# A retention layer and a gated FFN on one core: heads of odd pairs change places, and the products of the carried state go in two parts

## The chip, the cores and the metric

The kernel runs on one core of a Trainium2 chip. The metric is the device time of one launch in microseconds, as the median of several runs. The core has a matrix engine (TensorE, PE in the profile, with PEld for its weight loads), VectorE (DVE), ScalarE (ACT), GpSimd (POOL) and the sync engine (SP), which issues all transfers of this kernel on one queue that 16 DMA engines serve.

## The reference

Four sequences of 768 tokens, eight heads of 64 values. Each head carries a 64x64 state that decays by a fixed factor per token; the output of all heads, side by side, is the input x of a multiplicative FFN.

```python
q, k, v: (4, 8, 768, 64)          # batch, heads, tokens, head size
gamma = 1.0 - 2.0 ** (-5.0 - np.arange(H))
for t in range(S):
    state = gamma * state + outer(k[:, :, t], v[:, :, t])
    y[:, :, t] = scale * (q[:, :, t] @ state)
x = y.transpose(0, 2, 1, 3).reshape(B * S, H * D)      # 3072 x 512
a = x @ w1;  b = x @ w2                                # 512 x 1024 each
out = ((a * b) @ w3) @ w_out                           # 1024 x 1024, 1024 x 512
```

## The kernel before, in words

The tokens are cut into 12 stages of 256 (`n`), three to a sequence. W3 and w_out don't depend on the tokens, so the kernel first multiplies them into one 1024x512 matrix (`W3O`, functions `turn_w3`, `w3_mm`, `w3_out`). Everything is computed in float16 with float32 sums in PSUM.

A stage does this, and each step is a function. `load` brings Q, K and V of a stage into one of 15 staging buffers; `cast` and `cast_v` turn them into float16 (ScalarE the queries, GpSimd or VectorE the rest) and put a decay factor into V. Keys and queries are turned by TensorE in stages 0 to 2 and by a DMA transpose later (`dma_turn`, from stage 5 on `turn_pair` with both in one). `scores` are keys times queries inside chunks (two of 128 tokens in stages 0 and 1, four of 64 after), and `mask` cuts them to the causal part on VectorE. `kv` are keys times values, from which `state` makes the carried state at the start of each chunk, `TS[n, c]`. `inter` multiplies the carried state by the queries, and `av` adds scores times values to the same PSUM banks `X[n, 0]` and `X[n, 1]`. `x_out` takes them out with a decay factor into `XT[n]`, x transposed: row block `a` of 128 rows holds the pair of heads 2a and 2a+1. The FFN then computes `two_blocks` with W1 (`a_evac`, ScalarE) and W2 (`b_evac`, VectorE, which multiplies the two into `HT`), and `o_unit` multiplies `HT` by `W3O`; `o_copy` and `o_store` bring the result out. In stages 0 and 1 `rows` does the same as `two_blocks` in the order in which the blocks of W1 and W2 arrive.

All small products of a stage are 64x64: a product that reads its operands from partitions 0 to 63 or 64 to 127 uses the upper or lower half of TensorE's rows, and one that writes PSUM partitions 0 to 63 or 64 to 127 uses the left or right half of its columns. So there are four quarters. In `scores`, `kv` and `av` four products in a row lie on four quarters (`QUARTERS`). In `inter` before, the head r = 0 or 1 of a pair gives both halves (`X[n, g][half(r), ...]` from `TS[n, c][half(r), ...]`), so that two of the four quarters are in use. [...] In `inter` both row halves write both banks; in `av` row half g writes bank g. Between them stands `fence`: ScalarE reads a few elements of each bank, and `av` waits for it. From stage 4 on, the scores and keys-values of the next stage lie between `inter` and `av` of this one and cover that time.

The order on each engine is the order in which the program names the operations. It is written out by hand up to stage 3 (lines 588 to 853), with a loop after it (lines 902 to 942). A transfer whose staging buffer is in use, or whose semaphore still counts the transfer eight issues earlier, waits at the head of SP's queue, with all behind it.

Of the kernel before, what the change touches and what calls it, by code (L numbers as in the profile page):

```python
# [20 lines left out]
def kernel(  # L21
# [18 lines left out]
    PAIR = 3 + 2  # L40
# [15 lines left out]


# [62 lines left out]
    fetch(  # L120
        "r4 wo0 r1 r2 wo1 r5 wo2 r3 r6 k0 r7 wo3 q0 v0 r0 q1 k1 v1 w11 w13 w10 w12 w22 w23 w21 w20 "
        "v2 v3 k2 q2 k3 v4 q4"
    )
# [15 lines left out]
    def numbers():  # L139
# [6 lines left out]
        for h in range(H):  # L146
            r = (h % 2) * 64
            nc.gpsimd.memset(LGH[:, h : h + 1], -math.log(gam[h]))
            nc.gpsimd.memset(LGP[r : r + 64, h // 2 : h // 2 + 1], math.log(gam[h]))
# [73 lines left out]
    w3h, w3p, w3t, acc = {}, {}, {}, {}  # L223
# [23 lines left out]
    def w3_mm(f, i, tag=None, first=False, last=False):  # L247
        if first:
            acc[f] = bank(tag, [128, DM])
        for r in range(2):  # L250
# [6 lines left out]
    def w3_out(f, eng):  # L257
        copy(eng, W3O[f][:, :], acc.pop(f)[:, :])
# [116 lines left out]
    def kv(n, tags):  # L375
        last = n % PER == PER - 1
        if n < EO:
# [3 lines left out]
        for a in range(NP):  # L381
# [19 lines left out]

    def state(n, i, eng="g"):
        cs = chunks(n)
        if i == len(cs) and n % PER == PER - 1:
            return
# [22 lines left out]
    def inter(n, tags):  # L428
        begun = set()
        for g in range(2):  # L430
            X[n, g] = bank(tags[g], [128, NP, 128])
        cs = chunks(n)
        for a in range(NP):
            for c in cs:
                if (n, c) not in TS:
                    continue
                for r in range(2):
                    if n < EO:
                        g, o, rhs = c, X[n, c][half(r), a, :], qT[n][half(r), :, a, half(c)]
                    else:  # L440
                        s, g = c
                        o, rhs = X[n, g][half(r), a, s * 64 : (s + 1) * 64], qchunk(n, r, a, s, g)
                    nc.tensor.matmul(  # L443
                        o, lhsT=TS[n, c][half(r), a, :], rhs=rhs, start=((g, r) not in begun), stop=False,
                        skip_group_check=True,
                    )
                    begun.add((g, r))
        X[n] = begun

    def fence(n):  # L450

        for g in range(2):
            if (g, 0) in X[n]:
                s0 = 0 if n < EO or (n, (0, g)) in TS else 1
                t = att.tile([128, NP, 2 - s0], FP, tag=f"fence{g}", name="fence")
                nc.scalar.copy(t[:, :, :], X[n, g][:, :, :].rearrange("p a (s i) -> p a s i", s=2)[:, :, s0:, 0])  # L456

    def av(n):
        begun = X.pop(n)
        for a in range(NP):  # L460
            for t in range(2):
                for g, r in QUARTERS:
                    h = 2 * a + r
                    if n < EO:
                        o, rhs = X[n, g][half(r), a, :], am[n, a // 2, r][half(g), a % 2, t, :]
                    else:
                        o, rhs = X[n, g][half(r), a, t * 64 : (t + 1) * 64], am[n, None, r][half(g), a, t, :]
                    nc.tensor.matmul(  # L468
                        o, lhsT=v16[n][half(g), t, h * D : (h + 1) * D], rhs=rhs,
                        start=((g, r) not in begun), stop=(n >= EO or t == 1), skip_group_check=True,  # L470
                    )
                    begun.add((g, r))

    def x_out(n, g):
        if n not in XT:
# [19 lines left out]
    HT, pa = {}, {}  # L495

    def two_blocks(W, n, u, tag):
        ps = bank(tag, [128, 2, T])
# [13 lines left out]
    def b_evac(n, u, ps):  # L512
        if n not in HT:
            HT[n] = fsb.tile([128, 8, T], HP, tag="ht", name="ht", bufs=2)
        tt("v", HT[n][:, 2 * u : 2 * u + 2, :], pa.pop((n, u))[:, :, :], ps[:, :, :], MULT)
# [7 lines left out]
    rows_ps = {}  # L523

    def rows(W, n, uh, d, tags=None, first=False, last=False):

        w = "a" if W is W1 else "b"
        if first:
            rows_ps[w, n, uh] = [bank(t, [128, 2, T]) for t in tags]
        for j in range(4):  # L530
# [6 lines left out]
    def rows_out(w, n, uh, u, eng="s"):  # L537
        ps = rows_ps[w, n, uh][u]
# [7 lines left out]
    def o_unit(n, tb, tags, cuts=((0, 512),)):  # L546
        for (c0, c1), tag in zip(cuts, tags):
# [8 lines left out]
    o_sb = {}  # L556

    def o_copy(n, tb, c0=0, c1=512):
        if n not in o_sb:
            o_sb[n] = fsb.tile([128, 2, DM], FP, tag="osb", name="osb", bufs=3)  # L560
        nc.scalar.activation(o_sb[n][:, tb, c0:c1], o_ps.pop((n, tb, c0, c1))[:, :], AF.Copy, scale=final_scale)  # L561

    def o_store(n, tb, c0=0, c1=512):
        r0 = n * T + tb * 128
        nc.sync.dma_start(out[r0 : r0 + 128, c0:c1], o_sb[n][:, tb, c0:c1])  # L565

    def o_store_all(n):
        nc.sync.dma_start(
# [18 lines left out]
    ab = {}  # L587
    warm(8)
# [84 lines left out]
    w3_out(7, "s")  # L673
    turn("q", 1, "S1")
    mask(0, 1, 0)
    w3_out(6, "s")
    inter(0, ("S0", "X1"))
    cast("k", 1, "g")
    state(0, 2)
    fence(0)  # L680
    turned_w3(0, "v")
    av(0)
# [26 lines left out]
    inter(1, ("S1", "X0"))  # L709
    state(1, 2)  # L710
    rows(W1, 0, 1, 3)
    fence(1)
    state(1, 3)
    cast_w(W1, "w1", 2, "s")
    av(1)
    rows(W1, 0, 0, 0)
# [65 lines left out]
    inter(2, ("S1", "X0"))  # L782
    o_copy(0, 1)
    dma_turn("k", 3)
    fetch("q3 k4")
# [4 lines left out]
    fence(2)  # L790
    mask(2, 1)
    av(2)
# [10 lines left out]
    ab["a", 2, 0] = two_blocks(W1, 2, 0, "S1")  # L803
    o_copy(1, 1)
    state(3, 3)
    ab["a", 2, 1] = two_blocks(W1, 2, 1, "X0")
    state(3, 4)
    a_evac(2, 0, ab["a", 2, 0])
    cast("q", 3, "g")
    ab["a", 2, 2] = two_blocks(W1, 2, 2, "S0")  # L810
    a_evac(2, 1, ab["a", 2, 1])
# [4 lines left out]
    ab["a", 2, 3] = two_blocks(W1, 2, 3, "S1")  # L816
    a_evac(2, 2, ab["a", 2, 2])
    ab["b", 2, 0] = two_blocks(W2, 2, 0, "S0")
    cast("k", 4, "v")
    a_evac(2, 3, ab["a", 2, 3])  # L820
    ab["b", 2, 3] = two_blocks(W2, 2, 3, "S1")
    dma_turn("k", 4)
    fetch("q5 k5 v5")
    b_evac(2, 0, ab["b", 2, 0])
    ab["b", 2, 2] = two_blocks(W2, 2, 2, "X0")
    b_evac(2, 3, ab["b", 2, 3])
    ab["b", 2, 1] = two_blocks(W2, 2, 1, "S0")
    b_evac(2, 2, ab["b", 2, 2])
    inter(3, ("S1", "X1"))
    b_evac(2, 1, ab["b", 2, 1])  # L830
    scores(3, ("X0", "K"))
    fence(3)
# [5 lines left out]
    state(4, 2)  # L838
    av(3)
# [14 lines left out]

    LAST = 3

    def casts(n):
        if n < NS:  # L860
            cast("k", n, "g")
            cast_v(n, "g")

    def cast_queries(n):
        if n < NS:
            cast("q", n, "s")

    def turns(n):
        if n < NS:
            turn_pair(n)  # L870

    def loads(n):
        if n < NS:
            load("k", n)
            load("q", n, nc.sync)
            load("v", n, nc.sync)

    def catch_up(u):
        if u == 0:
            load("k", LAST + 3)  # L880
            turns(LAST + 2)
            o_store(2, 1)
            o_store(1, 1)
            o_store(2, 0)
            load("q", LAST + 3)
            load("v", LAST + 3)
        elif u == 1:
            load("k", LAST + 4)
        elif u == 3:
            casts(LAST + 3)  # L890

    def ahead(n):
        scores(n, ("S0", "S1"))
        kv(n, ("K", "F1"))

    def ahead_out(n):
        states(n)
        mask(n, 0)
        mask(n, 1)

    LATE = ()
    for n in range(LAST, NS):
        nxt = n + 1 < NS and n > LAST
        late = nxt and n in LATE
        if n > LAST:
            inter(n, ("X0", "X1"))
            fence(n)
            if nxt and not late:
                ahead(n + 1)
            av(n)  # L910
            x_out(n, 0)
            x_out(n, 1)
            if nxt and not late:
                ahead_out(n + 1)
            cast_queries(n + 2)
            turns(n + 2)
            if n == LAST + 1:
                load("q", n + 3)
                load("v", n + 3)
            loads(n + 4)  # L920
            casts(n + 3)
            o_unit(n - 1, 0, ("F2",))
            o_copy(n - 1, 0)
            o_unit(n - 1, 1, ("F0",))
            o_copy(n - 1, 1)
            o_store_all(n - 1)
        tags = ("F2", "F0", "X1" if late else "F1")
        for u in range(4):
            if late and u == 2:
                ahead(n + 1)  # L930
                for i in range(1, 4):
                    state(n + 1, i)
# [45 lines left out]
```

## Time and profile before

| | |
|---|---|
| median of 3 runs | 192.08 us (191.68 to 193.73) |
| span of the profiled execution | 190.6 us |
| PE busy | 174.9 us, 92% |
| PEld busy | 125.2 us, 66% |
| DVE busy | 100.6 us, 53% |
| ACT busy | 71.1 us, 37% |
| POOL busy | 50.5 us, 26% |
| moved by DMA | 40.75 MB, 214 GB/s in the mean |

The profile is one execution. The time of a run is longer than its span by launch and completion. Engine lines give a start and a length in microseconds, the engine, the line of the kernel, the operation with what it writes and reads, and how often it stands in a row; in brackets follows how long the engine stood idle before it and what ended that. In the chain, "DMA x" is a transfer from its issue to its landing. A busy PE is not a PE at its peak, since products overlap; so rates are read from the distance between starts.

### The profile page before, as it was taken

The page shows a single profiled execution, that of the slowest core. Times are in us where ns is not written, and L with a number is a line of the kernel's source. Part 1 is how long each engine was busy: PE and PEld are TensorE (multiplying, and loading weights), DVE is VectorE, ACT ScalarE, POOL GpSimd, SP SyncE. Part 2 cuts the span into 40 slices and gives each one's busy share as a digit, 9 for nine tenths or more (in the row PEclk, how much of TensorE's full clock was granted, in tenths as well). Part 3 has the DMA queues.
Part 4 walks back from the last instruction along what each step waited for, and adds up shares of the span by engine and source line. Part 5 has one row for each costly group of instructions (what it writes and reads, how often), then busy time and mean ns, then how long its engine had stood idle before and what let it go on. Part 6 is the DMA issues. An engine that isn't in the chain of part 4 may idle for free.

```text
span 190.6 us, 5952 instructions
## 1 busy us (share of the span) xinstructions
PE 174.9 (92%) x2592; PEld 125.2 (66%) x2592; DVE 100.6 (53%) x171; ACT 71.1 (37%) x131; POOL 50.5 (26%) x79
## 2 busy tenths in 40 slices
PE   7499998999999884899899969999999999999993
PEld 2254554788757652686785846868868688585872
DVE  2435788526866285538248427474384653744130
ACT  5634434462255202231534333343432432322322
POOL 7852237633230301020505233323033010000000
PEclk9979999999999999699999999999999999999999
DMA  5999999989998998999999999999998270030303
GB/s 218 399 407 357 321 290 381 413 210 235 234 212 185 206 246 179 223 252 241 203 219 193 291 198 243 237 246 229 216 292 215 39 185 3 0 115 0 108 6 110
DMA packets 83402, 40.75 MB, mean 214 GB/s; under 512 B 61232, under 2 KB 77872, under 8 KB 83376
## 3 DMA queue, kind: packets, MB, share of 16 engines
q1 hardware_dynamic: 83376, 40.38, 85.6%
q8 instruction: 20, 0.33, 0.8%
q14 instruction: 6, 0.05, 0.1%
HBM read 29.36 MB, written 6.29 MB: 187 GB/s over the span
## 4 chain that ended last, share of the span: by engine, by line
PE 57%; DMA 22%; SPq 6%; POOL 6%; issue 3%; DVE 2%; ACT 2%; POOLq 0%; DVEq 0%
PE psF L502 29%; PE psF L550 15%; DMA st<-in_k_dram 6%; DMA st<-in_v_dram 5%; DMA st<-in_moe_w_dram 4%; DMA st<-in_q_dram 4%; SPq L87 4%; DMA kqT<-kq 3%; PE psX L443 2%; PE psX L252 2%; PE psS L252 2%; SPq L565 1%; PE psX L468 1%; PE psS L353 1%; POOL v L62 1%
## 5 line engine op out<-in xcount | busy, mean ns | idle before, releaser
L502 PEld LDWEIGHTS <-w 128*128 128x128 f16 x640 | 63.3, 99 | 15.7 <-issue 5.8
L502 PE MATMUL psF<-xt,w 128*128 128x256 f16 x576 | 65.9, 276 | 4.0 <-ACT osb L561 4.0
L62 DVE TENSOR_TENSOR ht<-pa,psF 128x512 f16<-128x512 f32 x39 | 26.8, 687 | 42.3 <-PE psF L502 42.3
L550 PE MATMUL psF<-w3o,ht 128*128 128x512 f16 (+2 forms) x176 | 38.3, 370 | 0.0
L59 ACT COPY pa<-psF 128x512 f32<-128x512 f32 x39 | 22.7, 585 | 41.3 <-PE psF L502 36.6
L550 PEld LDWEIGHTS <-ht 128*128 128x128 f16 x200 | 18.4, 98 | 19.3
L62 POOL TENSOR_TENSOR v<-st,VN 128x1024 f16<-128x1024 f32 x8 | 15.2, 1902 | 33.3 <-DMA st<-in_v_dram 23.6
L561 ACT ACTIVATE osb<-psF 128x512 f32<-128x512 f32 (+2 forms) x22 | 12.6, 576 | 24.3 <-PE psF L550 24.3
L485 DVE TENSOR_TENSOR xt<-psX,YN 128x512 f16<-128x512 f32 x18 | 12.2, 725 | 8.8 <-PE psX L468 8.8
L532 PEld LDWEIGHTS <-w 128*128 128x128 f16 x128 | 12.1, 98 | 2.9 <-ACT w L59 1.3
L62 POOL TENSOR_TENSOR t<-s,GS 128x256 f16<-128x256 f32 x8 | 5.8, 726 | 30.5 <-DVE s L62 30.5
L252 PEld LDWEIGHTS <-w3t 128*128 128x128 f16 x64 | 5.8, 101 | 7.3 <-ACT w3t L59 1.6
L370 DVE TENSOR_TENSOR am<-psS,keep 128x512 f16<-128x512 f32 x15 | 9.6, 681 | 1.2 <-PE psX L353 1.2
L59 ACT CAST kq<-st 128x1024 f16<-128x1024 f32 x7 | 7.3, 1046 | 6.7 <-DMA st<-in_q_dram 6.7
L532 PE MATMUL psF<-xt,w 128*128 128x256 f16 x56 | 9.7, 273 | 0.0
L59 POOL CAST kq<-st 128x1024 f16<-128x1024 f32 x6 | 6.2, 1036 | 12.2 <-DMA st<-in_k_dram 12.2
L443 PEld LDWEIGHTS <-t 64*64 64x64 f16 x320 | 6.2, 109 | 3.1 <-issue 3.0
L240 PEld LDWEIGHTS <-w3h 128*128 128x128 f16 x64 | 4.4, 110 | 4.5 <-DVE w3h L59 3.5
L532 PE MATMUL psX<-xt,w 128*128 128x256 f16 x32 | 6.1, 273 | 0.8 <-ACT w L59 0.8
L502 PE MATMUL psS<-xt,w 128*128 128x256 f16 x48 | 5.7, 272 | 1.0 <-DVE ht L62 1.0
L468 PE MATMUL psX<-am,v 64*64 64x64 f16 (+1 forms) x320 | 6.0, 197 | 0.5 <-ACT fence L456 0.5
L468 PEld LDWEIGHTS <-v 64*64 64x64 f16 x384 | 5.0, 106 | 1.8 <-issue 0.9
(137 smaller groups left out, 201.3 us busy)
## 6 DMA issues: line engine op xcount, KB each, us to landing
st<-in_moe_w_dram SPq DMA_DIRECT2D x16, 512.0 KB, 8.9
st<-in_q_dram SPq DMA_DIRECT2D x12, 512.0 KB, 6.6
st<-in_v_dram SPq DMA_DIRECT2D x20, 256.0 KB, 5.9
st<-in_k_dram SPq DMA_DIRECT2D x20, 256.0 KB, 5.4
out_dram<-osb SPq DMA_DIRECT2D x8, 512.0 KB, 5.0
st<-in_moe_w_out_dram SPq DMA_DIRECT2D x4, 512.0 KB, 7.3
out_dram<-osb SPq DMA_DIRECT2D x7, 256.0 KB, 3.8
st<-in_k_dram SPq DMA_DIRECT2D x2, 512.0 KB, 10.1
```

The lines of the kernel that those rows point to most:

```text
L59: {"v": nc.vector.tensor_copy, "g": nc.gpsimd.tensor_copy, "s": nc.scalar.copy}[eng](dst, src)
L62: (nc.vector if eng == "v" else nc.gpsimd).tensor_tensor(dst, a, b, op)
L87: via.dma_start(t[:, s * 512 : (s + 1) * 512].rearrange("p (h d) -> p h d", d=D), src[:, s * 128 : (s + 1) * 128, :].rearrange("h i d -> i ...
L252: nc.tensor.matmul(acc[f][:, :], lhsT=w3t[f][:, g * 128 : (g + 1) * 128], rhs=WO[i][:, r, :], start=(first and r == 0), stop=(last and r = ...
L370: nc.vector.tensor_tensor(t[:, :, :, :].rearrange("p a s i -> p (a s) i"), ps[:, :, :, :].rearrange("p a s i -> p (a s) i"), keep64[:, :]. ...
L443: nc.tensor.matmul(o, lhsT=TS[n, c][half(r), a, :], rhs=rhs, start=((g, r) not in begun), stop=False, skip_group_check=True,)
L468: nc.tensor.matmul(o, lhsT=v16[n][half(g), t, h * D : (h + 1) * D], rhs=rhs, start=((g, r) not in begun), stop=(n >= EO or t == 1), skip_g ...
L485: nc.vector.tensor_tensor(XT[n][:, :, :].rearrange("p a (s x) -> p (a s) x", s=2)[:, :, g * 64 : (g + 1) * 64].rearrange("p k (i t) -> p k ...
L502: nc.tensor.matmul(ps[:, i, :], lhsT=W[d][:, f * 128 : (f + 1) * 128], rhs=XT[n][:, d, :], start=(i == 0 and d == 0), stop=(i == 1 and d = ...
L532: nc.tensor.matmul(rows_ps[w, n, uh][j // 2][:, j % 2, :], lhsT=W[d][:, f * 128 : (f + 1) * 128], rhs=XT[n][:, d, :], start=(first and j % ...
L550: nc.tensor.matmul(ps[:, :], lhsT=HT[n][:, f, tb * 128 : (tb + 1) * 128], rhs=W3O[f][:, c0:c1], start=(f == 0), stop=(f == 7),)
L561: nc.scalar.activation(o_sb[n][:, tb, c0:c1], o_ps.pop((n, tb, c0, c1))[:, :], AF.Copy, scale=final_scale)
```

## The change

Heads of odd pairs change places in the output. `place(a, r)` gives the half in which head r of pair a lies: its own for even a, the other for odd a. `inter` and `av` write there, `numbers` fills the decay table of x accordingly, and rows of W1 and W2 have to follow: blocks 1 and 3 (which multiply row blocks 1 and 3 of x) are loaded with their two halves exchanged, as two transfers of 64 rows.

`inter` is split into parts 0 and 1. In part 0 bank g takes its products from row half 1-g, in part 1 from row half g, as in `av`. So the fence moves between the two parts. It reads one element of one half of each bank. Within a part, the even and the odd pair together touch all four quarters. From stage 4 on the order is part 0, fence, half of the next stage's `kv`, its `scores`, the other half of `kv`, part 1, `av`. In stages 0 and 1 other products lie between the parts (in stage 0 the transposes of the queries of stage 1, in stage 1 two groups of `rows`), in stage 2 the scores and one output product, in stage 3 the scores, the keys-values of stage 4 and an output product. In the last stage the first output product of stage 10, now in two cuts of 320 and 192 columns, lies between them.

The output tiles of stages 0 and 1 are put into the buffers of the float16 w_out, and the loop is written out line by line. Apart from the lines shown, the order of the operations is kept.

```diff
+    def place(a, r):
+        return r ^ (a % 2)
...
+    def load_heads(src, i):
+        if i % 2 == 0:
+            return load_rows(src, i)
+        t = new_stage()
+        for r in range(2):
+            r0 = i * 128 + (1 - r) * 64
+            nc.sync.dma_start(t[r * 64 : (r + 1) * 64, :], src[r0 : r0 + 64, :])
+        return t
...
-                w_st[kind, i] = load_rows({"w1": moe_w1, "w2": moe_w2}[kind], i)
+                w_st[kind, i] = load_heads({"w1": moe_w1, "w2": moe_w2}[kind], i)
...
-    def kv(n, tags):
+    def kv(n, tags, parts=(0, 1)):
...
-        for a in range(NP):
+        for a in range(2 * parts[0], 2 * parts[-1] + 2):
...
+    def inter(n, part, tags=None):
...
+        for i in range(NP // 2):
+            for s in range(1 if n < EO else 2):
+                for a in (2 * i, 2 * i + 1):
+                    for g in range(2):
+                        c = g if n < EO else (s, g)
+                        if (n, c) not in TS:
+                            continue
+                        r = g ^ 1 ^ part
+                        o = place(a, r)
+                        if n < EO:
+                            dst, rhs = X[n, g][half(o), a, :], qT[n][half(r), :, a, half(c)]
+                        else:
+                            dst, rhs = X[n, g][half(o), a, s * 64 : (s + 1) * 64], qchunk(n, r, a, s, g)
+                        nc.tensor.matmul(
+                            dst, lhsT=TS[n, c][half(r), a, :], rhs=rhs, start=((g, o) not in begun), stop=False,
+                            skip_group_check=True,
+                        )
+                        begun.add((g, o))
...
     def fence(n):
-
         for g in range(2):
-            if (g, 0) in X[n]:
-                s0 = 0 if n < EO or (n, (0, g)) in TS else 1
-                t = att.tile([128, NP, 2 - s0], FP, tag=f"fence{g}", name="fence")
-                nc.scalar.copy(t[:, :, :], X[n, g][:, :, :].rearrange("p a (s i) -> p a s i", s=2)[:, :, s0:, 0])
+            if (g, g) in X[n]:
+                t = att.tile([128, 1], FP, tag=f"fence{g}", name="fence")
+                nc.scalar.copy(t[half(g), :], X[n, g][half(g), NP - 1, 64:65])
...
+    inter(4, 0, ("X0", "X1"))
+    fence(4)
+    kv(5, ("K", "F1"), (0,))
+    scores(5, ("S0", "S1"))
+    kv(5, ("K", "F1"), (1,))
+    inter(4, 1)
+    av(4)
...
+    inter(11, 0, ("X0", "X1"))
+    fence(11)
+    o_unit(10, 0, ("F2",), ((0, 320),))
+    o_copy(10, 0, 0, 320)
+    o_unit(10, 0, ("F1",), ((320, 512),))
+    inter(11, 1)
+    av(11)
+    o_copy(10, 0, 320, 512)
+    x_out(11, 0)
+    x_out(11, 1)
+    o_unit(10, 1, ("F0",))
```

More of the change, by code (lines that the diff above doesn't have):

```diff
@@ L426, in states @@
             state(n, i, eng)
-    def inter(n, tags):
-        begun = set()
-        for g in range(2):
[L431 to L448, printed above, removed]
@@ L673 @@
     w3_out(7, "s")
+    inter(0, 0, ("S0", "X1"))
+    fence(0)
     turn("q", 1, "S1")
@@ L892, in ahead @@
[L892 to L932, printed above, removed]
-                mask(n + 1, 0)
-            a_unit(n, u, tags[2 * u % 3])
-            b_unit(n, u, tags[(2 * u + 1) % 3])
-            if late and u == 2:
-                mask(n + 1, 1)
-            if late and u == 2 + 1:
-                state(n + 1, 4)
-                state(n + 1, 5)
-            if n == LAST:
-                catch_up(u)
@@ new lines @@
+    evac("a", 3, 2)
+    blk("b", 3, 2, "F1")
+    evac("b", 3, 2)
+    blk("a", 3, 3, "F2")
+    evac("a", 3, 3)
+    blk("b", 3, 3, "F0")
+    evac("b", 3, 3)
+    cast("k", 6, "g")
+    cast_v(6, "g")
+    inter(4, 0, ("X0", "X1"))
[5 more added lines that the diff above has]
+    av(4)
+    x_out(4, 0)
+    x_out(4, 1)
+    state(5, 1)
+    state(5, 2)
+    state(5, 3)
+    state(5, 4)
+    state(5, 5)
+    mask(5, 0)
@@ new lines @@
+    evac("a", 4, 2)
+    blk("b", 4, 2, "F1")
+    evac("b", 4, 2)
+    blk("a", 4, 3, "F2")
+    evac("a", 4, 3)
+    blk("b", 4, 3, "F0")
+    evac("b", 4, 3)
+    inter(5, 0, ("X0", "X1"))
+    fence(5)
+    kv(6, ("K", "F1"), (0,))
+    scores(6, ("S0", "S1"))
+    kv(6, ("K", "F1"), (1,))
+    inter(5, 1)
+    av(5)
+    x_out(5, 0)
+    x_out(5, 1)
+    state(6, 1)
+    state(6, 2)
+    state(6, 3)
+    state(6, 4)
+    state(6, 5)
+    mask(6, 0)
+    mask(6, 1)
+    cast("q", 7, "s")
+    turn_pair(7)
@@ new lines @@
+    evac("a", 5, 3)
+    blk("b", 5, 3, "F0")
+    evac("b", 5, 3)
+    inter(6, 0, ("X0", "X1"))
+    fence(6)
+    kv(7, ("K", "F1"), (0,))
+    scores(7, ("S0", "S1"))
+    kv(7, ("K", "F1"), (1,))
+    inter(6, 1)
+    av(6)
+    x_out(6, 0)
+    x_out(6, 1)
+    state(7, 1)
+    state(7, 2)
+    state(7, 3)
+    state(7, 4)
+    state(7, 5)
+    mask(7, 0)
+    mask(7, 1)
+    cast("q", 8, "s")
+    turn_pair(8)
+    load("k", 10)
+    load("q", 10)
+    load("v", 10)
+    cast("k", 9, "g")
@@ new lines @@
+    inter(7, 0, ("X0", "X1"))
+    fence(7)
+    kv(8, ("K", "F1"), (0,))
+    scores(8, ("S0", "S1"))
+    kv(8, ("K", "F1"), (1,))
+    inter(7, 1)
+    av(7)
+    x_out(7, 0)
+    x_out(7, 1)
+    state(8, 1)
+    state(8, 2)
+    state(8, 3)
+    state(8, 4)
+    state(8, 5)
+    mask(8, 0)
+    mask(8, 1)
+    cast("q", 9, "s")
+    turn_pair(9)
+    load("k", 11)
+    load("q", 11)
+    load("v", 11)
+    cast("k", 10, "g")
+    cast_v(10, "g")
+    o_unit(6, 0, ("F2",))
+    o_copy(6, 0)
@@ new lines @@
+    o_unit(6, 1, ("F0",))
+    o_copy(6, 1)
+    o_store_all(6)
+    blk("a", 7, 0, "F2")
+    evac("a", 7, 0)
+    blk("b", 7, 0, "F0")
+    evac("b", 7, 0)
+    blk("a", 7, 1, "F1")
+    evac("a", 7, 1)
+    blk("b", 7, 1, "F2")
+    evac("b", 7, 1)
+    blk("a", 7, 2, "F0")
+    evac("a", 7, 2)
+    blk("b", 7, 2, "F1")
+    evac("b", 7, 2)
+    blk("a", 7, 3, "F2")
+    evac("a", 7, 3)
+    blk("b", 7, 3, "F0")
+    evac("b", 7, 3)
+    inter(8, 0, ("X0", "X1"))
+    fence(8)
+    kv(9, ("K", "F1"), (0,))
@@ new lines @@
+    scores(9, ("S0", "S1"))
+    kv(9, ("K", "F1"), (1,))
+    inter(8, 1)
+    av(8)
+    x_out(8, 0)
+    x_out(8, 1)
+    state(9, 1)
+    state(9, 2)
+    state(9, 3)
+    state(9, 4)
+    state(9, 5)
+    mask(9, 0)
+    mask(9, 1)
+    cast("q", 10, "s")
+    turn_pair(10)
+    cast("k", 11, "g")
+    cast_v(11, "g")
+    o_unit(7, 0, ("F2",))
+    o_copy(7, 0)
+    o_unit(7, 1, ("F0",))
+    o_copy(7, 1)
+    o_store_all(7)
+    blk("a", 8, 0, "F2")
+    evac("a", 8, 0)
+    blk("b", 8, 0, "F0")
@@ new lines @@
+    evac("b", 8, 0)
+    blk("a", 8, 1, "F1")
+    evac("a", 8, 1)
+    blk("b", 8, 1, "F2")
+    evac("b", 8, 1)
+    blk("a", 8, 2, "F0")
+    evac("a", 8, 2)
+    blk("b", 8, 2, "F1")
+    evac("b", 8, 2)
+    blk("a", 8, 3, "F2")
+    evac("a", 8, 3)
+    blk("b", 8, 3, "F0")
+    evac("b", 8, 3)
+    inter(9, 0, ("X0", "X1"))
+    fence(9)
+    kv(10, ("K", "F1"), (0,))
+    scores(10, ("S0", "S1"))
+    kv(10, ("K", "F1"), (1,))
+    inter(9, 1)
+    av(9)
+    x_out(9, 0)
+    x_out(9, 1)
@@ new lines @@
+    state(10, 1)
+    state(10, 2)
+    state(10, 3)
+    state(10, 4)
+    state(10, 5)
+    mask(10, 0)
+    mask(10, 1)
+    cast("q", 11, "s")
+    turn_pair(11)
+    o_unit(8, 0, ("F2",))
+    o_copy(8, 0)
+    o_unit(8, 1, ("F0",))
+    o_copy(8, 1)
+    o_store_all(8)
+    blk("a", 9, 0, "F2")
+    evac("a", 9, 0)
+    blk("b", 9, 0, "F0")
+    evac("b", 9, 0)
+    blk("a", 9, 1, "F1")
+    evac("a", 9, 1)
+    blk("b", 9, 1, "F2")
+    evac("b", 9, 1)
+    blk("a", 9, 2, "F0")
+    evac("a", 9, 2)
@@ new lines @@
+    blk("b", 9, 2, "F1")
+    evac("b", 9, 2)
+    blk("a", 9, 3, "F2")
+    evac("a", 9, 3)
+    blk("b", 9, 3, "F0")
+    evac("b", 9, 3)
+    inter(10, 0, ("X0", "X1"))
+    fence(10)
+    kv(11, ("K", "F1"), (0,))
+    scores(11, ("S0", "S1"))
+    kv(11, ("K", "F1"), (1,))
+    inter(10, 1)
+    av(10)
+    x_out(10, 0)
+    x_out(10, 1)
+    state(11, 1)
+    state(11, 2)
+    state(11, 3)
+    state(11, 4)
+    state(11, 5)
+    mask(11, 0)
+    mask(11, 1)
+    o_unit(9, 0, ("F2",))
+    o_copy(9, 0)
```

350 lines of the change are left out of this document (267 added, 83 removed).

## The prediction

> **What bounds the kernel now.** I read the chain of work that ended last first, then the 40 slices, then the timelines of TensorE and of the DMA queue. The chain (start, us, what):
>
> ```profile
> 25.05 7.52 DMA st<-in_moe_w_dram
> 32.59 1.05 ACT w L59
> 33.69 0.39 PE psX L532 x2
> ...
> 43.46 5.80 DMA st<-in_k_dram
> ...
> 68.37 7.07 DMA st<-in_q_dram
> ...
> 90.87 0.60 ACT osb L561
> 91.51 7.15 PE psF L502 x64
> ...
> 106.55 6.21 DMA kqT<-kq
> 112.81 0.45 PE psS L353 x32
> 113.52 0.27 PE psX L468 x32
> 113.79 3.56 PE psF L550 x16
> 117.34 6.99 PE psF L502 x64
> 124.33 0.56 PE psX L443 x28
> ```
>
> Until 112.81 us the chain returns to a transfer again and again: a block of W1, K, Q, and last the transposed keys and queries of stage 7, for which TensorE stands 1.67 us. From there to 187 us it runs on TensorE alone, in a period of 12 us: the products of the carried state (L443), scores (L353), keys-values (L392), `av` (L468), the output product (L550), the two FFN products (L502). The slices agree:
>
> ```profile
> PE   7499998999999884899899969999999999999993
> DMA  5999999989998998999999999999998270030303
> ```
>
> The DMA engines are 80 to 99% busy up to slice 31 (about 148 us). So there are two regimes. Before 112.8 us TensorE's savings end in a longer wait for a transfer, and a microsecond of DMA work is a microsecond of the result. After it the reverse holds, as the DMA then runs ahead: the transposes of stages 8 to 11 land 1 us or more before their scores.
>
> **Gain: the products of the carried state.** TensorE's timeline at stage 7 and at stage 11, the last:
>
> ```profile
> 124.26 0.63 PE L443 MATMUL psX<-kqT,t 64*64 64x64 f16 x28
> ...
> 124.79 0.42 PE L353 MATMUL psS<-kqT 64*64 64x64 f16 x28
> ...
> 172.17 0.69 PE L443 MATMUL psX<-kqT,t 64*64 64x64 f16 x32
> 172.93 0.25 ACT L456 COPY fence<-psX 128x8 f32<-128x8 f32 x2 [0.94 <-PE psX L443]
> 173.15 0.52 PE L468 MATMUL psX<-am,v 64*64 64x64 f16 x32 [0.28 <-ACT fence L456]
> ```
>
> Stage 7's 32 state products (28 in the first line, four mixed with the first scores) run from 124.26 to 124.79; less four scores that run in between, 0.49 us, or 15.5 ns each. They use two of the four 64x64 quarters: rows r go to columns r. Scores use all four, and 32 of them fill 112.81 to 113.08, 8.5 ns each. In the new order four products in a row (bank 0 and 1 of an even pair, then of an odd one) fall on the four quarters, so I price them at 8.5 ns: 32 x 8.5 = 0.27 us, a gain of 0.22 at stages 7, 8 and 10. Stage 9 opens a sequence and has 24 products: 0.37 becomes 0.20, gain 0.17.
>
> The fence must not show. At stage 11, where nothing covers it, 0.47 us pass from the start of the last state product (172.67 in the trace) to the first `av` at 173.15. The new cover is a half of the keys-values, the scores and the other half: 64 products (56 where a sequence ends), 0.54 to 0.51 us. It holds by 0.04 us at the least, and a miss costs its excess, at most 0.05 a stage. The two copies shrink from 8 elements on 128 partitions to one on 64; an 8- and a 4-element copy both took about 0.165, so I book nothing.
>
> Stage 11 gets another cover: the output product of stage 10 (first block, 1.75 us) moves between the halves. From the first state product to the output product 1.43 us pass now (172.17 to 173.60). Then: 0.14 + 0.14 for the halves, 0.46 for `av` and its hand-over, 0.20 for one more change between 64-wide and 128-wide products and back (the first state product starts 0.20 after the last FFN product's start, 0.09 beyond that one's pitch), 0.02 for cutting 512 columns into 320 and 192 (the same cut in the last stage: 16 products in 1.74 us, 8 whole ones 1.73). That is 0.96, gain 0.47. What this cover held before: the two x copies of stage 11 (0.73 each, about 1.70 to the end with the wait) now lie under one output block of 1.73, so it just fits; 0.05 at risk. The block needs the last H of stage 10, which VectorE ends at 173.04 and the product reaches at 173.25.
>
> Stage 6 gains only 0.03: its first half and the first half of keys-values run inside the wait for the transpose, the rest after it (96 products as before). Stages 0 to 5 gain nothing: what they save is waited for at 33.7, 77.1, 91.5 and 112.8 us. That also swallows the two more changes of width at stages 0 and 1 (0.2 each) and the state products of stage 0, which now wait for the state before the transposes of Q. Together: 3 x 0.22 + 0.17 + 0.47 + 0.03 = 1.3 us.
>
> **No cost, one sentence each.** The place of heads in x and LGP is another address in the same instructions. The output tiles of stages 0 and 1 lie in the buffers of w_out, last read before 33 us and first overwritten after 50. The loop written out keeps the order of SP, ACT, POOL and VectorE outside the lines named; the DMA queue differs in the next point alone.
>
> **Cost: four weight loads in halves.** Blocks 1 and 3 of W1 and of W2 come as two transfers of 64 rows instead of one of 128. The queue has 12 issues for 8:
>
> ```profile
> 25.05 5.71 SPq L95 DMA_DIRECT2D st<-in_moe_w_dram  x8
> 32.63 9.89 SPq L87 DMA_DIRECT2D st<-in_v_dram  x4
> ```
>
> The issue itself is 0.38 us where nothing holds it, four more 1.5 us, inside the 1.87 us between the eighth issue's end (30.76) and the next (32.63), which waits for a landing. Behind these issues stand V and K of stages 2 and 3; with eight transfers in flight, some 7 us deep, none of them starves. What is open is the rate. The whole loads land one every 1.28 us (32.56, 33.83, 35.11, 36.39 in the trace's landings): 512 KB at 410 GB/s, 16 engines each writing eight rows of 4 KB at 159 ns. They have nothing in reserve. No row shows a transfer into 64 partitions. Lower bound: a half takes half, 0.64 us, cost 0. [...] Other 256 KB transfers (K and V) land every 1.0 to 1.1 us, and that would be 8 x 0.43 = 3.4, but their rows are 256 bytes. [...]
>
> [...]
>
> All of the cost counts. The first half-loaded block is the one TensorE waits for at 33.69, and everything in the queue behind it shifts: K of stage 2 (landing at 49.3, on the chain), Q of stages 5 and 6, the transpose at 112.8.
>
> **The sum.** The profiled execution's span is 190.6 us; the median of the three runs is 192.08, 1.5 above it, launch and spread. I add the difference to the median: 192.1 + 2.6 - 1.3 = 193.4 us, no change within the 1% that a measurement of this kernel can tell (its three runs lie 1.1% apart).
>
> **Rivals.**
> [...]
> 2. The halves cost nothing. Then 192.1 - 1.3 = 190.8. If the earlier state products also pull transfers forward (buffers freed sooner at stages 2 to 6, five times 0.22), 189.7. For it: same bytes, same 4 KB rows. Against: no row with 64 partitions.
> 3. The new order isn't faster: the quarters are not filled at 8.5 ns because consecutive products share a row half or a bank. Then only stage 11's wait for the fence, 0.28, is saved: 192.1 + 2.6 - 0.3 = 194.4. For it: state products read their weights from many small tiles. Against: `av` and scores, of the same shape, already run at 8 to 9 ns.
>
> **Chances.** Forecast 0.38 (a cost of 1.4 to 3.2, so 192.2 to 194.0, its own range), rival 1 0.27, rival 2 0.27, rival 3 0.08. Slower by over 1%: rivals 1 and 3, 0.35. Faster by over 1% (under 190.2): the lower part of rival 2, 0.15. Within 1%: 0.50. The range reaches from the middle of rival 2 to rival 1 with a little for fences that show: 189.9 to 196.1.
>
> **What would show it.** Right: L477's 32 state products in two groups of about 0.14 us, `av` without a wait for the fence, 1.2 us from the first state product to the output product at stages 7, 8 and 10; W1's first block landing near 33.2 instead of 32.6 and the last W2 block near 44.5 instead of 41.9; the transpose of stage 7 near 115.4. [...] A fence wait over 0.05 us per stage, or state products over 12 ns, make the gain wrong; a late shift that does not reach 112.8 makes wrong that the DMA bounds that whole stretch.

## The result, and the profile after

The changed kernel takes 198.67 us (median; 196.82 to 199.93), the kernel before 192.38 beside it on the same chip: a ratio of 1.033, interval 1.026 to 1.040. Ratios, here and below, leave out runs more than 1.5% above the fastest of their kernel. It is slower by 6.3 us, where 193.4 and a range up to 196.1 had been forecast. The profiled execution took 199.28, its span is 197.6.

The chain of work that ended last (start, us, what) now stands on the weight loads for 20 us without a break, where one of 7.52 us stood before:

```profile
28.11 8.61 DMA st<-in_moe_w_dram
36.73 11.63 DMA st<-in_moe_w_dram
...
113.47 6.38 DMA kqT<-kq
...
149.41 6.71 DMA kqT<-kq
```

And there is a second transposed block on it, at 149.41, late in the stretch in which TensorE had run alone before. The slices of the page show the same place. Each slice is 4.9 us, so 29 to 49 us are the seventh to the tenth. The last line is that of the kernel before, with slices of 4.8 us:

```profile
PE   7489999585999989599899967999999899999993
DMA  6999999999899999998999999999998591020303
GB/s 215 386 402 353 323 276 217 299 204 192 195 234 236 171 206 247 239 228 237 230 165 259 214 230 247 240 236 260 152 263 197 157 163 49 3 109 2 109 0 106
...
GB/s 218 399 407 357 321 290 381 413 210 235 234 212 185 206 246 179 223 252 241 203 219 193 291 198 243 237 246 229 216 292 215 39 185 3 0 115 0 108 6 110
```

The DMA engines are as busy as before (9s), but move 217, 299 and 204 GB/s in slices 7 to 9, where the kernel before moved 381, 413 and 210. Busy at a lower rate means that each piece takes longer. A descriptor is the piece of a transfer that one engine moves at a time, here a row of 4 KB: it took 159 ns before (the median, 28 to 42 us), and takes 276 ns on average between 29 and 49 us, 304 in the seventh slice and 323 in the ninth. That loss is carried through to the end almost unchanged. The last W2 block lands at 49.50 instead of 41.92 (7.6 later), the transpose of stage 7 at 119.85 instead of 112.76 (7.1), and the span is 7.0 longer.

TensorE at stage 7 and at stage 11, the last:

```profile
131.34 0.32 PE L477 MATMUL psX<-kqT,t 64*64 64x64 f16 x16
...
131.76 0.33 ACT L489 COPY fence<-psX 64x1 f32<-64x1 f32 x2 [0.60 <-PE psX L477]
...
132.01 0.45 PE L477 MATMUL psX<-kqT,t 64*64 64x64 f16 x16
...
132.27 0.44 PE L504 MATMUL psX<-am,v 64*64 64x64 f16 x32
132.64 0.11 PEld L598 LDWEIGHTS <-ht 128*128 128x128 f16 x2
```

```profile
179.47 0.32 PE L477 MATMUL psX<-kqT,t 64*64 64x64 f16 x16
...
179.72 1.92 PE L598 MATMUL psF<-w3o,ht 128*128 128x320 f16 x16
...
181.57 0.32 PE L477 MATMUL psX<-kqT,t 64*64 64x64 f16 x16
...
181.71 0.43 PE L504 MATMUL psX<-am,v 64*64 64x64 f16 x32
```

The first 16 state products start at 131.34 and give way to the next kind 0.148 us later, 9.2 ns each, where they took 15.5 before and 8.5 had been forecast. The trace gives these products as tiles of 64x64, those of the FFN as 128x128, but not the quarter on which one lies: that the four quarters fill is read from this distance. The second 16 take 0.26 (132.01 to `av` at 132.27), not 0.14: in the trace the first of them, in bank 0, starts at 132.01, the second, in bank 1, only at 132.14, and the other 14 follow within 0.12. The first fence copy ends at 131.91, the second at 132.09, so bank 1 waits for the second copy. From the first state product to the output product 1.30 us pass, 1.43 before, 1.2 forecast. TensorE's period is 11.85 us instead of 11.97. At stage 11, with a whole output block as cover, nothing waits, and the last stage from its first state product to TensorE's end is 14.97 instead of 15.52.

So the new order does gain, and the loads lose far more. The experiments ask three things: what makes the loads slow, what the order is worth without them, and why less than its own sum comes out at the end.

### The profile page after: what moved, and what is told of

Its sections match the earlier page's. It is cut to its first block, busy times and chain, and to the rows that moved or that the text cites. A ratio compares the mean times of both kernels' runs of the same rounds, so it can differ in the third digit from the quotient of the medians.

```text
span 197.6 us, 5974 instructions
## 1 busy us (share of the span) xinstructions
PE 176.5 (89%) x2600; PEld 124.9 (63%) x2600; DVE 99.8 (51%) x171; ACT 73.1 (37%) x132; POOL 50.4 (26%) x79
## 4 chain that ended last, share of the span: by engine, by line
PE 52%; DMA 33%; DVE 4%; SPq 3%; issue 2%; ACT 2%; POOL 2%; DVEq 0%; POOLq 0%; ACTq 0%
PE psF L543 27%; PE psF L598 14%; DMA st<-in_moe_w_dram 14%; DMA kqT<-kq 7%; DMA st<-in_q_dram 7%; DMA st<-in_k_dram 6%; PE psS L264 2%; PE psX L477 2%; DVE ht L65 2%; PE psX L264 2%; PE psS L366 1%; PE psX L504 1%; SPq L85 1%; SPq L90 1%; ACT osb L616 1%
## 5 line engine op out<-in xcount | busy, mean ns | idle before, releaser
L598 PEld LDWEIGHTS <-ht 128*128 128x128 f16 x208 | 19.1, 98 | 18.6
L616 ACT ACTIVATE osb<-psF 128x512 f32<-128x512 f32 (+2 forms) x21 | 11.6, 556 | 25.4 <-PE psF L598 25.3
L578 PE MATMUL psX<-xt,w 128*128 128x256 f16 x32 | 6.6, 291 | 5.5 <-ACT w L62 3.3
L477 PEld LDWEIGHTS <-t 64*64 64x64 f16 x320 | 5.3, 106 | 4.4 <-issue 3.7
L366 PE MATMUL psS<-kqT 64*64 64x64 f16 x224 | 3.4, 196 | 3.6 <-DMA kqT<-kq 3.6
L264 PE MATMUL psS<-wo,w3t 128*128 128x512 f16 x16 | 5.6, 475 | 1.1 <-ACT w3t L62 1.1
```

The source lines that it names most:

```text
L264: nc.tensor.matmul(acc[f][:, :], lhsT=w3t[f][:, g * 128 : (g + 1) * 128], rhs=WO[i][:, r, :], start=(first and r == 0), stop=(last and r = ...
L366: nc.tensor.matmul(ps[r][half(g), a, s, :], lhsT=kT[n][half(r), s, a, half(g)], rhs=qchunk(n, r, a, s, g), start=True, stop=True,)
L477: nc.tensor.matmul(dst, lhsT=TS[n, c][half(r), a, :], rhs=rhs, start=((g, o) not in begun), stop=False, skip_group_check=True,)
L578: nc.tensor.matmul(rows_ps[w, n, uh][j // 2][:, j % 2, :], lhsT=W[d][:, f * 128 : (f + 1) * 128], rhs=XT[n][:, d, :], start=(first and j % ...
L598: nc.tensor.matmul(ps[:, :], lhsT=HT[n][:, f, tb * 128 : (tb + 1) * 128], rhs=W3O[f][:, c0:c1], start=(f == 0), stop=(f == 7),)
L616: nc.scalar.activation(o_tile(n, tb)[:, c0:c1], o_ps.pop((n, tb, c0, c1))[:, :], AF.Copy, scale=final_scale)
```

## The experiments

**The two parts of the change, each alone.** First the changed kernel with whole loads; the exchange of rows is left out, so blocks 1 and 3 multiply the wrong rows of x:

```
-                w_st[kind, i] = load_heads({"w1": moe_w1, "w2": moe_w2}[kind], i)
+                w_st[kind, i] = load_rows({"w1": moe_w1, "w2": moe_w2}[kind], i)
```

> The changed kernel, but blocks 1 and 3 of W1 and W2 are loaded whole, as before; the exchange of their rows is left out. Theory A (transfers into 64 partitions are slow, and that alone makes the change slow): the W2 block 0 lands near 42 us again, the scores of stage 7 start near 112.8, and the time is that of before less the gain of the new order, 191.0 to 191.9. Rival B (four more transfers on the queue are slow, whatever their shape): the same here. Rival C (the new order of stages 0 to 3 delays the transfers): still 197 to 199.

Measured: 0.987 of the kernel before (0.983 to 0.991), from three runs; a longer measurement is below. Then the kernel before with the half loads and nothing else:

```
+    def load_halves(src, i):
+        if i % 2 == 0:
+            return load_rows(src, i)
+        t = new_stage()
+        for r in range(2):
+            nc.sync.dma_start(t[r * 64 : (r + 1) * 64, :], src[i * 128 + r * 64 : i * 128 + (r + 1) * 64, :])
+        return t
```

> The kernel before with one edit: blocks 1 and 3 of W1 and W2 come as two transfers of 64 rows, rows in their old place. A and B: last W2 block lands near 49 instead of 41.9, the time is 198.5 to 199.5. C: no change, 192.4.

Measured: 1.030 (1.023 to 1.036), 5.7 us. That is most of the loss, without any exchange of heads and without the new order. A transfer lands in 16 parts, one for each DMA engine. From the first W1 block to the first V block (the first part of each) 15.1 us pass instead of 10.1. The last W2 block lands at 46.41, not near 49 as expected.

**Is it the number of transfers, or the 64 rows?** The same four blocks in two transfers of half the columns, 128 rows of 2 KB:

```
-            nc.sync.dma_start(t[r * 64 : (r + 1) * 64, :], src[i * 128 + r * 64 : i * 128 + (r + 1) * 64, :])
+            nc.sync.dma_start(t[:, r * 512 : (r + 1) * 512], src[i * 128 : (i + 1) * 128, r * 512 : (r + 1) * 512])
```

> The kernel before, and the same four blocks in two transfers each, but cut by columns: 128 partitions of 2 KB. As many transfers of the same size as with 64 rows. A: no change, 192.0 to 192.9, last W2 block near 42. B: 198 to 199.5.

Measured: 1.000 (0.995 to 1.006); the halves land 0.65 us apart, half of a whole block's 1.28. As many transfers, issues and bytes as with 64 rows, and no cost in the time. Its one profile, of a run of 194.67 us, is less clean: the last W2 block lands at 43.88 there, not near 42. The throughput line of the page, first of the 64-row run and then of this one, shows the difference in its eighth and ninth slices (316 and 242, then 408 and 318):

```profile
GB/s 218 407 398 353 321 278 272 316 242 183 194 249 167 246 231 254 191 251 257 199 194 215 260 187 258 238 229 258 198 214 261 90 200 3 0 113 0 107 4 108
```

```profile
GB/s 219 358 411 358 325 272 263 408 318 178 180 210 171 268 230 217 203 272 246 177 236 191 289 187 260 234 244 235 201 292 232 38 190 3 0 114 0 110 2 109
```

Then all eight blocks in 64-row halves (`if i % 2 == 0` taken out):

> The kernel before with all eight blocks of W1 and W2 in two transfers of 64 rows: the price of one split block. A with a plain doubling (1.28 us per block): 192.4 + 8 x 1.28 = 202.6. A with the 1.75 us per block that the changed kernel shows (7 us over four): 206.4. If the whole loads between the halves are what is slow beyond doubling, then with no whole loads left the price falls to 1.28 per block. C: 192.4.

Measured: 1.038 (1.030 to 1.047), 7.4 us for eight blocks against 5.7 for four. The halves land a steady 1.04 us apart. This is less than the lowest price expected (1.28 us a block), and not proportional: four halved blocks among whole ones cost 1.4 us each, eight in a row 0.92 each.

**Which rows?** Blocks 1 and 3 in three transfers, of rows 0-31, 32-95 and 96-127:

```
+        for p0, p1 in ((0, 32), (32, 96), (96, 128)):
+            nc.sync.dma_start(t[p0:p1, :], src[i * 128 + p0 : i * 128 + p1, :])
```

> The kernel before, with blocks 1 and 3 of W1 and of W2 in three transfers each, of rows 0-31, 32-95 and 96-127, to the same rows; nothing else changed. [...] Theory A2 (any transfer of 64 rows is slow, wherever it lies): the 64-row one takes 1.04, each 32-row one 0.5 or more, 0.76 or more per block: at least the 5.7 us of the two-halves run, 198 or more.

Measured: 1.024 (1.013 to 1.036) from two runs, less than A2 expects (198 us, 1.029), with an interval that holds it. The 32-row transfers land 0.52 to 0.66 us apart, the middle ones 0.93 to 1.27, where half of a whole block's time is 0.64. In this kernel the three sorts overlap, so the run can't tell whether the middle rows are slow or their neighbours slow them. The cost had to be measured by itself: groups of 12 transfers with nothing beside them, and a drain in between.

```
    # 2 rows 0-63
        rows(i, 0, 64)
...
    # 3 rows 32-95
        rows(i, 32, 64)
...
    # 4 the two halves by turns
        rows(i, (i % 2) * 64, 64)
...
    # 6 every second row
        put(tiles[i][0:128:2, :], blocks[i][0:64, :])
...
    # 8 64 rows of the source on 128 partitions
        put(tiles[i][:, 0:512], blocks[i][0:64, :].rearrange("r (j c) -> (r j) c", j=2))
```

> Loads alone, no attention and no FFN (the output is zeros): ten groups of 12 transfers of weight rows, each group let end before the next starts. In microseconds from one landing to the next. Whole blocks (128 rows of 4 KB): 1.28. [...] Theory S (the source sets the rate, 64 rows read in one piece against 128): 64 source rows on 128 partitions 1.04, and 128 half rows on 64 partitions 0.65. [...] The last group has the order of the changed kernel (halves, halves, three whole, halves, halves, whole): 12.5 by a sum of the pieces (8 x 1.04 + 4 x 1.28 = 13.4 less the first landing), 15 if whole blocks beside halves are slowed as in the run with halves alone.

The table of stretches, one inside each group's steady part (from:to, length, VectorE, GpSimd, clock, DMA busy share, GB/s). In order: whole blocks, rows 0-63, rows 32-95, halves by turns, column halves, every second row, rows 0-31, 64 source rows on 128 partitions, 128 half rows on 64 partitions, the changed kernel's order:

```profile
11.00:20.00 9.00, 2.79 (x4) 0.00 (x0) 1.00 1.02 415
27.00:37.00 10.00, 0.00 (x0) 0.00 (x0) 1.00 1.04 210
47.00:51.00 4.00, 0.00 (x0) 0.00 (x0) 1.00 0.97 369
59.00:69.00 10.00, 0.00 (x0) 0.00 (x0) 1.00 1.05 239
79.00:82.00 3.00, 0.00 (x0) 0.00 (x0) 1.00 1.05 402
94.00:96.00 2.00, 0.00 (x0) 0.00 (x0) 1.00 0.93 350
102.00:107.00 5.00, 0.00 (x0) 0.00 (x0) 1.00 1.04 207
116.00:119.00 3.00, 0.00 (x0) 0.00 (x0) 1.00 1.05 398
128.00:138.00 10.00, 0.00 (x0) 0.00 (x0) 1.00 1.07 210
144.00:157.00 13.00, 0.00 (x0) 0.00 (x0) 1.00 1.03 295
```

Read down the last column: 415, 402, 398 wherever 128 partitions are written; 210, 207, 210 wherever only partitions 0-63 (or 0-31) are; 369 and 350 for 64 partitions that lie in both halves. Their descriptors are back at 159 ns (median), and most of their landings are 0.6 to 0.7 us apart, near the pace of the issues (one every 0.64). The source doesn't matter: 64 rows read in one piece run at 398 when written to 128 partitions, and 128 half rows read at 210 when written to 64. So the partitions written set the rate in these groups. Theory S fails, and so does A2 of the run before (64 rows slow wherever they lie). Rows 0-63 take 1.25 us a half, as long as a whole block's 1.27: half the rate, and more than the 1.04 that a half took with all eight blocks in halves. Two halves by turns take 1.12 each, so they overlap by a tenth (239 GB/s against 210).

Another expectation failed: in the last group whole blocks beside halves are not slowed. There they land 1.28 us after what is ahead of them, the halves 1.12, 13.0 in all from first to last.

**What the order of products is worth.** The changed kernel with whole loads again, in more runs, and the same with the last stage as before:

> The changed kernel with whole loads of W1 and W2 once more (rows of blocks 1 and 3 left unexchanged, so their products take other rows of W), in more rounds and beside the three above: it was 0.987 of the kernel before from three runs, while the same kernel with the last stage as before was 1.002 from eleven. Theory H (the last stage is worth 0.55 to 0.6 us, the three runs were lucky): 0.996 to 0.999. Rival J (the last stage holds 2 us or more): 0.985 to 0.99.

```
-    o_unit(10, 0, ("F2",), ((0, 320),))
-    o_copy(10, 0, 0, 320)
-    o_unit(10, 0, ("F1",), ((320, 512),))
     inter(11, 1)
     av(11)
-    o_copy(10, 0, 320, 512)
     x_out(11, 0)
     x_out(11, 1)
+    o_unit(10, 0, ("F2",))
+    o_copy(10, 0)
```

> The changed kernel with whole loads (the exchange of rows in blocks 1 and 3 left out, so that its products take other rows of W), and with the last stage as before: the output product of stage 10 stands behind av of stage 11 again, whole; the two parts of stage 11's state products then stand next to each other with the fence bare. That run without this edit was 0.987 of the kernel before, 2.4 us. Theory H (the last stage is worth what its own trace shows, 0.55): 190.7, 0.990; the other 1.9 us were gained earlier. Rival J (the last stage holds most of the gain, since the rest is hidden by transfers): 191.8 or more, 0.996 or over.

Measured: 0.997 (0.993 to 1.001) for the first, so the 0.987 was mostly luck; 1.002 (0.998 to 1.006) for the second, measured at another time. The traces are finer than these times. From stage 7's first state product to TensorE's end the kernel before takes 63.43 us and the kernel with whole loads 62.35: 1.08 gained. The last stage alone takes 15.52 before, 14.97 with its cover, and 15.67 with the new order but no cover. So the moved output block is worth 0.70, and the new order without cover costs 0.15 there: theory H. The time of the second run is over what H expected (0.990, itself reckoned from the lucky 0.987) and by its number alone would speak for J; the traces are what decides for H.

**Does the exchange have to be paid?** Whole loads, rows exchanged by the casts (the four added calls of the second function are left out here):

```
+        if d % 2 == 0:
+            copy(eng, W[d][:, :], w_st[st, d][:, :])
+        else:
+            copy(eng, W[d][half(0), :], w_st[st, d][half(1), :])
...
+        copy(eng, W[d][half(1), :], w_st[st, d][half(0), :])
```

> The changed kernel with whole 128-row loads of W1 and W2; the exchange of rows of blocks 1 and 3 is made by the casts to 16 bit instead: each of these four blocks is cast in two halves, rows 64-127 to rows 0-63 and back, on two engines. Complete computation. Theory A (the half transfers were all of the loss): about 190 us, 0.985 to 0.992 of the kernel before, like the run with whole loads and rows left unexchanged (0.987); the last W2 block lands near 42 to 43 us, the transpose of stage 7 near 112.7. Rival D (the exchange has a price wherever it is made): four casts more, some of them on VectorE ahead of the first FFN products, push stage 0 back by 1 us or more: 191.5 to 192.5, with PE waiting for a cast at 34 to 42 us.

Measured: 1.005 (1.000 to 1.009), over what A expected; the median, 191.8 us, lies in D's range. The 3% are back, the order's gain is not: this version is no faster than the kernel before. D's sign is there too: TensorE waits 0.85 us up to 34.01 for a cast of ScalarE, and the kernel with whole loads has no such wait there. The timeline of ScalarE shows a price that A had not counted: a cast of 64 partitions takes as long as one of 128 (1.04 and 1.05 us).

```profile
32.41 1.04 ACT L62 CAST w<-st 64x1024 f16<-64x1024 f32 x1 [0.59 <-DMA st<-in_moe_w_dram]
...
36.60 1.05 ACT L62 CAST w<-st 128x1024 f16<-128x1024 f32 x1
```

**The second part's 0.26 us.** In the profile after, the two fence copies run one behind the other (0.33 us); before they overlapped (0.25). This kernel lets them read 2 or 4 elements instead of one from stage 2 on, on top of the last:

```
-                nc.scalar.copy(t[half(g), :], X[n, g][half(g), NP - 1, 64:65])
...
+                    nc.scalar.copy(
+                        t[half(g), :, :],
+                        X[n, g][half(g), :, :].rearrange("p a (s i) -> p a s i", s=2)[:, 1::2, s0:, 0],
+                    )
```

> The kernel of the row above, with the two fence copies of stages 2 to 11 reading 2 or 4 elements on 64 partitions instead of one. Complete computation. Theory F (the copies of one element run one behind the other on ScalarE, 0.33 us together, and that is why the second part of the state products takes 0.22 to 0.26 us instead of 0.15): with more than one element they overlap again as before the change (0.25 us together), the second part shrinks to 0.15 to 0.18, and stages 7 to 11 gain 0.08 each: 0.3 to 0.5 us under the row above. Rival G (their order comes from what they wait for, not from their size): the same start-to-start distance of 0.18 us and the same time within 0.2 us.

```profile
123.22 0.34 ACT L494 COPY fence<-psX 64x4 f32<-64x4 f32 x2 [0.55 <-PE psX L477]
```

Measured: 0.998 (0.994 to 1.003), 1.2 us under the run above by the ratios, with intervals that overlap. The copies still run one behind the other, so F's reason is wrong. They start 0.37 us after stage 7's first state product instead of 0.42, and the period becomes 11.80 instead of 11.85: a gain of 0.05 a stage, 0.08 expected. What orders the copies stays open. No run leaves the fence out, so its need is not shown. But this profile shows where such gains go:

```profile
148.20 0.45 PE L366 MATMUL psS<-kqT 64*64 64x64 f16 x32 [1.32 <-DMA kqT<-kq]
```

The transpose of stage 10 is late by 1.3 us here, which takes more than the order had gained by then.

**More room for the transposes.** On top of that kernel, the stores of stages 3 to 7 are issued behind the transposes of stages 7 to 11, not ahead of them; then the same in the kernel before:

```
     o_copy(3, 1)
-    o_store_all(3)
...
     turn_pair(7)
+    o_store_all(3)
```

> The kernel with casts that exchange rows and wider fence copies, and with the stores of the outputs of stages 3 to 7 each issued behind the transposes of stages 7 to 11 instead of ahead of them. Complete computation. Theory K (from stage 7 to 10 the DMA has no more slack than TensorE had: its transposes come at the end of a full queue, so a faster TensorE only waits longer for them): the transposes land up to 1.3 us earlier, one store of 512 KB; the waits at stage 7 (1.4 us) and stage 10 (0.3 to 1.4 us) shrink, and the time falls by 1 to 2.5 us, to 0.985 to 0.993 of the kernel before. Rival L (the stores fill a gap in which the transposes wait for their cast anyway): within 0.3 us of the same kernel without the move (0.998).

> The kernel before with the same stores behind the transposes, nothing else changed. Complete computation. Theory K: its only late wait, 1.67 us at stage 7, shrinks by up to 1.3: 0.993 to 0.998 of the kernel before; what the row above has over this one is then the new order of products without the wait that ate it, 1.0 to 1.3 us. Rival L: no change, 0.999 to 1.001.

Measured: 0.986 (0.979 to 0.993) and 0.992 (0.988 to 0.996). The first is the fastest complete version, 2.6 us under the kernel before. SyncE's own timeline shows the exchanged issues, at stage 7:

```profile
104.32 4.43 SPq L317 DMA_TRANSPOSE kqT<-kq  x1
108.79 0.58 SPq L635 DMA_DIRECT2D out_dram<-osb  x1
```

The wait of the scores falls to 0.7 us at stage 7 (1.4 in the kernel without the move) and 0.4 at stage 10 (1.3). That fits K, but single traces don't show it: at stage 10 the version with exchanging casts, without the move, waits only 0.27 us, and the kernel before with the move 0.48, where it had not waited at all. The transposes didn't land 1.3 us earlier, either: issued 1.9 us earlier, stage 7's lands 0.64 earlier (110.72, 111.36). And the gain of the move in the kernel before is not explained by K: from stage 5 on its one trace takes 89.34 us, as the kernel before did (89.10). That trace is ahead by 1.6 us already at stage 5 (97.01 instead of 98.59), before the place of the first moved store (104.75). Where its 1.5 us come from stays open, and so does what the order is worth between these two runs (0.6%, with intervals that overlap).

## Why the prediction was wrong

**The step that failed is the term of the half loads**: 2.6 us were booked, and they cost 5.7 alone (halves in the kernel before) and about 6.9 in the changed kernel (1.033 against 0.997 with whole loads, of 192). No run shows the 2.6: it was an estimate, half of the 5.1 us that eight halves cost if each takes a whole block's 1.28 us instead of 0.64 (8 x 0.64). The mark of the prediction for the first W1 block was 33.2 us; it landed at 35.47. Two things were mis-sized.

First, half of the 5.1 was taken, as if a half were slow only half of the time. The loads alone show the opposite: 1.25 us with the same half each time, a whole block's time to 2%, and 1.12 by turns. The parts of a transfer land within 0.4 to 0.8 us there. By turns, a block then costs 2 x 1.12 - 1.27 = 0.97, and four cost 3.9, not 2.6. With a wider spread it is little less: with all eight blocks in halves the parts of a transfer lie 2.5 to 2.9 us apart, more than two halves, and a half still takes 1.04 us, where half of the 5.1 would be 0.96.

Second, the 5.1 itself was no upper limit. It took the whole blocks beside the halves to keep their 1.28 us. In the changed kernel the first parts of whole blocks follow what is ahead of them after 2.00, 1.73, 1.28 and 2.08 us, in all 2.0 more than four times 1.28. Those of the halves follow after 1.1 to 1.45, in all 5.1 more than eight times 0.64, so the halves alone cost the whole 5.1 there. From the first W1 block to the first V block this makes 17.5 us instead of 10.1. Alone, in the same order, nothing of the kind is seen. One difference is the step of the engines: there the 16 parts of a transfer land within 0.4 to 0.6 us; in the changed kernel 4.3 us lie between the first and the last part of the first half, in the kernel with halves alone 2.7. That this slows the whole blocks is not shown. No run set the step of the engines; 13 of the 16 parts of that first half land within 1.0 us; and with whole loads the spread at the same place is 1.5 to 2.4, so it may be an effect of the halves as well as a cause. The loads alone also lack the K, Q and V transfers around the weights. And with column halves, which cost nothing in the time, one whole block also follows after 1.70 us. So the cause of this part stays open.

**Rival 1**, with the whole 5.1 us for the halves (192.1 + 5.1 - 1.3 = 195.9), was nearer, and too low for that second reason: with 5.1 the last W2 block would land near 47, and it landed 2.5 us later.

**That all of the cost counts** was right: 7.6 us at the last W2 block, 7.1 at stage 7, 7.0 in the span.

**The gain** was right in kind and a fifth too large over the late stages. Forecast were 0.22 a stage; 0.125 came. The first half shrank as forecast (9.2 ns a product). The step that failed there is "the fence must not show": the second half takes 0.22 to 0.26 instead of 0.14, some 0.1 a stage where at most 0.05 was allowed, because the second copy follows the first: from the last product of part 0 to the first one of part 1 in bank 1 it takes 0.68 us at stage 7, not the 0.47 read at stage 11 of the kernel before. Stage 11 gained 0.55 (0.47 forecast). Together 1.08 from stage 7 on, 1.3 forecast. Rival 3 is refuted: four quarters give 9.2 ns a product, two gave 15.5.

**That the DMA runs ahead after stage 7** was right for the kernel before and too much for the new one. The transpose of stage 10 landed at 146.16 before, over 2 us early. In six profiles with the new order and the stores in their old place its scores wait in four: 0.69 us in the changed kernel, 0.27 to 1.32 in others. The kernel with whole loads waits 1.31 in one of its two profiles and not at all in the other, which is the second line here:

```profile
156.17 0.45 PE L366 MATMUL psS<-kqT 64*64 64x64 f16 x32 [0.69 <-DMA kqT<-kq]
```

```profile
146.52 0.45 PE L366 MATMUL psS<-kqT 64*64 64x64 f16 x32
```

So the DMA bound can reach to stage 10, and part of what TensorE gains there can be waited away, by an amount that differs from run to run. The 1.08 us in TensorE's timeline are 0.6 in the time, but the interval (-0.1 to 1.3) holds 1.08 too, so the times don't show that loss.

## What to carry to other kernels

When a load is split, look at which partitions each piece writes, not at its bytes or the number of transfers: a split by columns cost nothing, a split into rows 0-63 and 64-127 cost 0.9 to 1.7 us a block. If rows must change places and the DMA is the bound, pick pieces that lie in both halves (369 GB/s for rows 32-95 against 210 for rows 0-63, shown with the loads alone only; no run tried an exchange with them, or in one transfer), or do it in a later instruction and count that one in full: here it used up the gain. A saving in the engine that sets the pace can be waited away at the next resource (here the transpose of stage 10, over 2 us early before, was late by 0.27 to 1.32 us in four profiles of six): measure by how much the transfers are early before booking it.

## What was not expected of the hardware

- 64 partitions are loaded nearly as fast as 128 if they lie in both halves: 369 GB/s for rows 32-95 and 350 for every second row, against 210 for rows 0-63 and 415 for all 128, each with rows of 4 KB.
- Whole blocks queued between halves follow up to 0.8 us later in the kernel (2.08 instead of 1.28) and no later alone; the cause is open.
- A cast of 64x1024 takes 1.04 us on ScalarE, the same as one of 128x1024.
- Copies of 1 or of 4 elements on 64 partitions run one behind the other on ScalarE (0.33 us for two), where two copies of 8 elements on 128 partitions overlapped (0.25); the cause is open.
